# Fused attention and MLP, forward and backward in one kernel: W3 read ahead of the V prefetch, W4 in a V buffer, half of dW4 later

## The chip, the cores and the metric

One core of one Trainium2 chip. Its engines run their own instruction streams in order and meet through semaphores: PE (TensorE, matrix products into the accumulator memory PSUM; the load of its weights is shown as PEld), DVE (VectorE), ACT (ScalarE), POOL (GpSimd) and SP (SyncE). SP and POOL do almost no arithmetic here: SP issues the reads from memory into the on-chip memory, POOL issues the writes back. All transfers run on the same 16 DMA engines. The metric is device time in microseconds.

## The reference

A block for one token (D = 640) is run forward and then differentiated. Attention has 32 heads, a cache of 8192 keys and values for each and 192 numbers per key; the MLP has 1536 hidden units.

```python
def _A_ref(x, k_cache, v_cache, wq, wo):
    q = (x @ wq).reshape(B, Sq, Hq, Dh).transpose(0, 2, 1, 3)
    scores = jnp.einsum('bhqd,bhkd->bhqk', q, k) * Dh ** (-0.5)
    o = jnp.einsum('bhqk,bhkd->bhqd', _softmax(scores), v)
    return o.transpose(0, 2, 1, 3).reshape(B, Sq, Hq * Dh) @ wo
...
mod = (_silu(c) @ w_mod).reshape(c.shape[0], 6, 1, -1)
sa, ca, ga, sb, cb, gb = ...
h = _layernorm(x) * (1 + ca) + sa
x = x + ga * _A_ref(h, A_k_cache, A_v_cache, A_wq, A_wo)
h = _layernorm(x) * (1 + cb) + sb
x = x + gb * _B_ref(h, B_w1, B_w2, B_w3, B_w4)
...
_out, _vjp = jax.vjp(_f, A_x, A_k_cache, A_v_cache, A_wq, A_wo, B_w3, B_w4, c, w_mod)
return (_out, *_vjp(grad_out))
```

With one token the shifted branch inside `_B_ref` is zero, so the MLP part is `x1 + gelu(layernorm(x1) @ w3) @ w4`. Ten results are written: the block's output and the gradients of x, the K cache, the V cache, wq, wo, W3, W4, c and w_mod. The gradients of the two caches are as large as the caches (out_2 and out_3, 100 MB each), so most of the bytes are K and V in, V in once more, dK and dV out.

## The kernel before

A head's K or V is read as two tiles of 128 partitions x 32 keys x 192 numbers (1536 KB each), called (head, half). Three parts follow one another.

**Forward, heads 0 to 31** (the loop at L582, one step works on three heads at once). K is multiplied by q (`fwd_mult`), summed over the 192 numbers by PE (`fwd_ssum`), the softmax weights E are made (`fwd_exp`), K is scaled by E on ACT and DVE (`fwd_scale`, L394 and L402), and PE multiplies V with the scaled K, with a last column for E itself (`fwd_kvA`, `fwd_kvB`, L419 and L427). This gives the output of the head and a matrix that later yields the gradient of q without a further read of K. `fwd_keep` and `fwd_keepB` copy that matrix from PSUM into `MA` and `MB`; `fwd_kvK` (L435) adds the scaled K into one accumulator, kb_ps.

**The turn** (L662 to about L955). The last head's output goes through wo, the layer norm, W3, the gelu and W4, and back again to `dao_bf` (L924), the gradient of the attention's output. Only then can any gradient of a cache be made. The backward step through W3 needs W3 transposed, which PE does in 60 blocks (`w3T_some`, L678, copied from PSUM by ACT or DVE into w_t3 and w_t2); `u_mm` (L742) is the forward product with W3. `dg_some` (L143 in the trace) makes the row sums of W4 times the incoming gradient, twelve `dot`s on DVE. `dw4_some` (L816) makes the twelve blocks of W4's gradient on DVE. `woT_some` transposes the last rows of wo; `do_half` turns dao_bf into `do_pb`, the gradient of the last pair of heads' outputs.

**Backward, heads 31 to 0** (the loop at L1263; `HS` is the list of heads in that order). For each head V is multiplied by do_pb (`bwd_mult`, L131), summed by PE (L1056), dK is made by DVE (`bwd_dk`) and dV by ACT and DVE (`bwd_dv`); PF and P2h are the softmax weights, made by `bwd_pf_act` on ACT and `bwd_pf_dve` on DVE. Beside each head run jobs: `J1` holds a list per step (dwo, dW3, later wq and w_mod). `ring_load` issues the V reads as their buffers come free: a read waits for the last use of what was in the buffer. `bwd_ttr` (L985) multiplies wo's rows with dao, for the heads to come.

Buffers: `big` has five tiles, shared by K, part of the weights, and the outputs dK and dV; `fv` has three for V; `fpr` two, for the products of K and then for V; `bso` two for small outputs. A tile is reused when its last reader, a transfer too, is done.

W4 and W3 lie in three tiles, w_t0 (nine of W4's twelve blocks), w_t1 (three of W4's blocks and two of W3's five) and w_t2 (three of W3's five blocks); w_t3 takes transposed blocks. Before, all four are `big` tiles. The order of PE, DVE and ACT is pinned to the order of the program text; SP and POOL follow their program order as well. At the end of the forward loop the reads on SP stand in this order: V(30,0), V(30,1), V(31,0), W4 (nine blocks), V(31,1), wo, V(29,0), V(29,1), W4 (three blocks), W3 (two blocks), V(30,0) again, W3 (three blocks), V(30,1) again; then wo rows for the backward heads and the ring of V reads. V(31,0) and V(31,1) stay in their tiles from forward to backward.

On POOL, the writes start with the first six blocks of dW4, the two parts of dV(31,0), two writes of three dW4 blocks each, dV(31,1), dV(30,0), dV(30,1), dK(31,0), dK(31,1).

The lines on which the steps depend:

```python
        if i == HQ:
            V_b[HQ - 3] = [load_v(fpr, HQ - 3, t) for t in range(2)]
            alloc_wt(1)
            load_wt(1)
            V_b[HQ - 2] = [load_v(fv, HQ - 2, 0)]
            alloc_wt(2)
            load_wt(2)
            V_b[HQ - 2].append(load_v(big, HQ - 2, 1))
            dg_some(0, 7)
```

## Time and profile before

| | |
|---|---|
| median of 3 runs | 1402.19 us (1401.65 to 1403.26) |
| profiled execution | 1402.17 us, span 1400.4 us |
| busy share of the span | PE 61%, PEld 48%, DVE 77%, ACT 68%, POOL 8% |
| moved | 570.81 MB, 408 GB/s over the span |
| read, written | 343.08 MB, 225.91 MB |

Times in the profile are microseconds from the start of the span. A row of a timeline gives the start, the length, the engine, the line of the program, the operation, the tiles it writes and reads with their shapes, how many instructions are merged in the row, and in brackets how long the engine stood idle before it and what ended that wait. SPq rows are the issue of a transfer, not the transfer; a long one was held by its queue. A row of stretches gives, for each engine, the busy time and the number of instructions, then the granted TensorE clock (1.00 is full speed), the mean busy share of the 16 DMA engines and the rate in GB/s. A share can come out slightly over 1.

### The profile page before, as it was taken

The numbers are of one execution on the slowest core, as the hardware profiler recorded it, in microseconds if no ns is written. First come the engines' busy times: TensorE is split into PE (matmuls) and PEld (weight loads), VectorE is DVE, ScalarE is ACT, GpSimd is POOL, SyncE is SP. The second block draws the span as 40 slices with busy tenths as digits, with TensorE's granted clock in tenths as the row PEclk, the third lists the DMA queues.
The fourth block names the chain that finished last, engine by engine and source line by source line (L and its number), as shares of the span: only waits on it lengthen the run. The fifth ranks groups of instructions, "written<-read, shape, count | busy, mean of one in ns | idle before, by whom it ended". The sixth has DMA issues, their size and how long they took to land. (4 is left out here: it accounts for less than half of the span.)

```text
span 1400.4 us, 28087 instructions
## 1 busy us (share of the span) xinstructions
PE 851.4 (61%) x11512; PEld 670.5 (48%) x11512; DVE 1084.7 (77%) x1328; ACT 952.1 (68%) x2603; POOL 111.3 (8%) x202
## 2 busy tenths in 40 slices
PE   3799999999999997554657454332343443534240
PEld 3577777777777776443546343222232232323230
DVE  3678888887878886599988986777577678779794
ACT  1578887787877775575875786565666558559680
POOL 0000000000000000101110101111111111111011
PEclk9799999999999999666666657665667666666575
DMA  9999999999999999588999999999999999999997
GB/s 393 418 420 418 418 420 419 420 420 420 419 408 420 411 417 381 193 340 337 425 427 424 428 426 428 427 428 427 426 427 425 425 425 418 426 418 423 429 429 303
DMA packets 73168, 570.81 MB, mean 408 GB/s; under 512 B 6863, under 2 KB 19919, under 8 KB 32591
## 3 DMA queue, kind: packets, MB, share of 16 engines
q1 hardware_dynamic: 48736, 343.10, 59.5%
q0 software_dynamic: 24272, 225.92, 38.3%
q8 instruction: 90, 1.47, 0.4%
q14 instruction: 40, 0.32, 0.1%
q10 hardware_dynamic: 30, 0.00, 0.0%
HBM read 343.08 MB, written 225.91 MB: 406 GB/s over the span
## 5 line engine op out<-in xcount | busy, mean ns | idle before, releaser
L1074 ACT ACTIVATE dV<-do_pb,PF 128x192 bf16<-128x192 bf16 x1248 | 435.1, 440 | 80.3 <-DMA out_dram<-dK 64.9
L1056 PE MATMUL dP_ps<-V_sb,ident_bf 128*128 128x256 bf16 x1536 | 228.2, 323 | 239.9 <-DVE V_sb L131 239.9
L394 ACT ACTIVATE EK<-K_sb,E_f 128x192 bf16<-128x192 bf16 x1024 | 363.5, 442 | 8.8 <-PE kb_ps L435 3.1
L1056 PEld LDWEIGHTS <-ident_bf 128*128 128x128 bf16 x1536 | 177.4, 116 | 290.3 <-issue 171.9
L1041 DVE TENSOR_TENSOR dK<-dS,q_pb 128x6144 bf16<-128x6144 bf16 (+1 forms) x67 | 213.0, 3211 | 37.9 <-DMA out_dram<-dK 34.1
L131 DVE TENSOR_TENSOR prod<-K_sb,q_pb 128x6144 bf16<-128x6144 bf16 x64 | 214.6, 3354 | 35.4 <-DMA K_sb<-in_A_k_cache_dram 35.0
L131 DVE TENSOR_TENSOR V_sb<-V_sb,do_pb 128x6144 bf16<-128x6144 bf16 x64 | 211.9, 3350 | 6.0 <-DMA V_sb<-in_A_v_cache_dram 6.0
L419 PE MATMUL ps_a<-EK,V_sb 128*128 128x193 bf16 x2048 | 199.2, 250 | 23.1 <-DMA V_sb<-in_A_v_cache_dram 22.2
L419 PEld LDWEIGHTS <-V_sb 128*128 128x128 bf16 x2048 | 173.1, 99 | 43.0 <-DMA V_sb<-in_A_v_cache_dram 35.0
L402 DVE TENSOR_TENSOR EK<-K_sb,P2h 128x1536 bf16<-128x1536 bf16 x128 | 121.6, 951 | 0.0
L1041 DVE TENSOR_TENSOR dV<-P2h,do_pb 128x2304 bf16<-128x2304 bf16 (+1 forms) x63 | 85.0, 1375 | 45.2 <-DMA out_dram<-dV 40.0
L427 PE MATMUL ps_b<-EK,V_sb 128*64 128x193 bf16 x2048 | 111.3, 251 | 0.0
L361 PE MATMUL S_ps<-prod,ident_bf 64*64 64x256 bf16 x3072 | 100.7, 279 | 9.5 <-DVE prod L131 9.1
L361 PEld LDWEIGHTS <-ident_bf 64*64 64x64 bf16 x3072 | 84.2, 110 | 24.7 <-issue 24.1
L427 PEld LDWEIGHTS <-V_sb 128*64 128x64 bf16 x2048 | 83.6, 110 | 21.0 <-issue 21.0
L382 ACT ACTIVATE E_f<-sm_ps,negm 128x64 f32<-128x64 f32 x32 | 10.0, 314 | 83.1 <-DVE negm L380 83.1
L435 PE MATMUL kb_ps<-EK,hot_bf 128*32 128x384 bf16 x1024 | 66.0, 335 | 0.0
L1080 POOL DMA_DIRECT2D out_dram<-dV x63 | 33.7, 535 | 392.4 <-ACT dV L1074 255.5
L194 ACT CAST do_pb<-bc_ps 128x384 bf16<-128x384 f32 x15 | 7.1, 470 | 78.2 <-PE bc_ps L190 78.2
L1161 PEld LDWEIGHTS <-ident_bf 128*128 128x128 bf16 x112 | 15.2, 136 | 93.3 <-issue 91.8
L1095 POOL DMA_DIRECT2D out_dram<-dK x67 | 37.0, 553 | 192.0 <-DVE dK L1041 153.8
L1125 ACT ACTIVATE wq_o<-wq_bc,ha_f 128x1536 bf16<-128x1536 bf16 x12 | 18.5, 1566 | 49.4 <-DMA out_dram<-wq_o 49.4
(317 smaller groups left out, 828.9 us busy)
## 6 DMA issues: line engine op xcount, KB each, us to landing
V_sb<-in_A_v_cache_dram SPq DMA_DIRECT2D x126, 1536.0 KB, 16.8
K_sb<-in_A_k_cache_dram SPq DMA_DIRECT2D x64, 1536.0 KB, 19.0
out_dram<-dV POOLq DMA_DIRECT2D x63, 1536.0 KB, 21.9
out_dram<-dK POOLq DMA_DIRECT2D x63, 1536.0 KB, 22.3
wq<-in_A_wq_dram SPq DMA_DIRECT2D x3, 2560.0 KB, 34.1
wo_t<-in_A_wo_dram SPq DMA_DIRECT2D x16, 480.0 KB, 18.3
out_dram<-dwo POOLq DMA_DIRECT2D x16, 480.0 KB, 19.9
wq<-in_A_wq_dram SPq DMA_DIRECT2D x4, 1920.0 KB, 36.0
```

The lines of the kernel that those rows point to most:

```text
L131: nc.vector.tensor_tensor(out=out, in0=a, in1=b, op=ALU.mult)
L361: nc.tensor.matmul(st["S_ps"][c0 : c0 + 64, r, t * JH : (t + 1) * JH, :], lhsT=ident_bf[64 * r : 64 * r + 64, 64 * r : 64 * r + 64], rhs=p ...
L394: nc.scalar.activation(out=EK[:, jj, 0:DH], in_=K_st[h, t][:, r * JQ + jj, :], func=ACT.Copy, scale=st["E_f"][:, j : j + 1])
L402: nc.vector.tensor_tensor(out=EK[:, NA:JQ, 0:DH].rearrange("p j (d r) -> p j d r", r=2), in0=K_st[h, t][:, r * JQ + NA : (r + 1) * JQ, :]. ...
L419: nc.tensor.matmul(st["A_ps"][:, 0 : DH + 1], lhsT=V_sb[:, r * JQ + jj, a0:a1], rhs=EK[:, jj, 0 : DH + 1], start=(q == 0 and jj == 0), sto ...
L427: nc.tensor.matmul(st["B_ps"][g : g + 64, 0 : DH + 1], lhsT=V_sb[:, r * JQ + jj, b0:b1], rhs=EK[:, jj, 0 : DH + 1], start=(q == 0 and jj < ...
L435: nc.tensor.matmul(kb_ps[g : g + 32, 0 : 2 * DH], lhsT=hot_bf[:, HQ - 1 - h : 2 * HQ - 1 - h], rhs=EK[:, jj : jj + 2, 0:DH], start=(h == 0 ...
L1041: nc.vector.tensor_tensor(out=o.rearrange("p j (d r) -> p j d r", r=2), in0=pairs[:, :, None, :].to_broadcast([P, n, NP2, 2]), in1=vec.rea ...
L1056: nc.tensor.matmul(bst[h]["dP_ps"][:, t * JH : (t + 1) * JH, :], lhsT=ident_bf, rhs=V_sb[:, :, k * DS : (k + 1) * DS], start=(k == 0), sto ...
L1074: nc.scalar.activation(out=o[:, jj, :], in_=doh, func=ACT.Copy, scale=bst[h]["PF"][:, j0 + jj : j0 + jj + 1])
L1080: st2.dma_start(out=dV_hd[h][:, j0 + r0 : j0 + r1, :], in_=o[:, r0:r1, :])
L1095: st2.dma_start(out=dK_hd[h][:, j0 : j0 + n, :], in_=o[:, r0 : r0 + n, :])
```

## The change

- **Reads.** W4's nine blocks go into the `fv` buffer that V(31,0) had, and are read ahead of V(31,0), which goes into `big`. In the last forward step the rest of W4 and all of W3 are read first, and the four V tiles for the backward part after them. The order on SP becomes V(30,0), V(30,1), W4 (nine), V(31,0), V(31,1), wo, W4 (three), W3 (two), W3 (three), V(29,0), V(29,1), V(30,0), V(30,1).
- **Row sums of W4.** `dg_some` makes four at the first place and eight at the second, instead of seven and five.
- **Kept matrices.** `fwd_keep` is split. For the last head the copies into MA, Bt and MB stand later, beside the products with W3. The last head's four `fwd_kvK` groups, which stood together between the transposes, are spread: one ahead of `u_mm`, three in the tail. Two groups of eight transposes are copied by DVE instead of one, and the first of them comes as soon as du_bf is made.
- **dW4.** Six of the twelve blocks stay in the turn, with one write. The other six become two jobs, `job_dw4`, of backward steps 22 and 23, on ACT, each with a write of three blocks.
- **PF of the second head** is made on ACT together with the first one's, before `woT_some`, instead of after `bcast_dao`.
- **x's gradient columns.** `job_mid`, with the block's output, goes from step 1 to step 11; `mid_cols` from step 1 to step 2; the result of W4's product is copied from PSUM (h2_c) at step 0.

```diff
@@ -332,7 +332,7 @@
 
     def fwd_load(h, t):
         if 0 <= h < HQ and len(st[h]["V"]) == t:
-            st[h]["V"].append(load_v(big if (h, t) == (HQ - 2, 1) else fv, h, t))
+            st[h]["V"].append(load_v(big if (h, t) in ((HQ - 2, 1), (HQ - 1, 0)) else fv, h, t))
         if h + 2 < HQ and (h + 2, t) not in K_st:
             K_st[h + 2, t] = load_k(h + 2, t)
 
@@ -453,16 +453,21 @@
         k = int(2 * hp >= H_LO)
         return mm_parts[k][2][:, hp - k * H_LO // 2, :]
 
+    def fwd_keepA(h, st):
+        nc.scalar.copy(out=MA(h), in_=st["A_ps"][:, 0 : DH + 1])
+
+    def fwd_keepBt(h, st):
+        _, _, bp, _, _ = head_split(h)
+        Bt = fsm.tile([P, DH + 1], FP32, name="Bt")
+        nc.scalar.copy(out=Bt[bp : bp + 64, :], in_=st["B_ps"][64 - bp : 128 - bp, 0 : DH + 1])
+        st["Bt"] = Bt
+
     def fwd_keep(h, st):
         if h == H_LO:
             kx_cm.__exit__(None, None, None)
             mm_open("mm_hi", HQ - H_LO)
-        (a0, a1), (b0, b1), bp, ca_, cb_ = head_split(h)
-        op = 64 - bp
-        nc.scalar.copy(out=MA(h), in_=st["A_ps"][:, 0 : DH + 1])
-        Bt = fsm.tile([P, DH + 1], FP32, name="Bt")
-        nc.scalar.copy(out=Bt[bp : bp + 64, :], in_=st["B_ps"][op : op + 64, 0 : DH + 1])
-        st["Bt"] = Bt
+        fwd_keepA(h, st)
+        fwd_keepBt(h, st)
 
     def fwd_keepB(h, st):
         (a0, a1), (b0, b1), bp, ca_, cb_ = head_split(h)
@@ -528,7 +533,7 @@
         return w_t[f // W4_N][:, c0 + lo : c0 + hi]
 
     def alloc_wt(k):
-        w_t.append(flat(big_tile(f"w_t{k}")))
+        w_t.append(flat(ring_tile(fv) if k == 0 else big_tile(f"w_t{k}")))
 
     def load_wt(k):
         if k < 2:
@@ -590,18 +595,16 @@
         if p:
             fwd_wo(i - 1, st[i - 1])
         if i == HQ - 1:
-            fwd_load(HQ - 1, 0)
             alloc_wt(0)
             load_wt(0)
+            fwd_load(HQ - 1, 0)
         if i == HQ:
+            for k in (1, 2):
+                alloc_wt(k)
+                load_wt(k)
             V_b[HQ - 3] = [load_v(fpr, HQ - 3, t) for t in range(2)]
-            alloc_wt(1)
-            load_wt(1)
-            V_b[HQ - 2] = [load_v(fv, HQ - 2, 0)]
-            alloc_wt(2)
-            load_wt(2)
-            V_b[HQ - 2].append(load_v(big, HQ - 2, 1))
-            dg_some(0, 7)
+            V_b[HQ - 2] = [load_v((fv, big)[t], HQ - 2, t) for t in range(2)]
+            dg_some(0, 4)
         if pp:
             fwd_kv(i - 2, 2, st[i - 2])
         if c:
@@ -658,7 +661,7 @@
             fwd_o_head(HQ - 2)
             dve_copy(o_col_bf[:, NQC - 3 : NQC - 2], o_col_f[:, NQC - 3 : NQC - 2])
             dve_copy(o_col_bf[0:64, NQC - 2 : NQC - 1], o_col_f[0:64, NQC - 2 : NQC - 1])
-            dg_some(7, NFC)
+            dg_some(4, NFC)
     w_t.append(flat(big_tile("w_t3")))
     NB3 = JH * DH // P
 
@@ -712,10 +715,8 @@
     dot(jk, xs, xs, s3[:, 1:2])
     dot(jk, xs, cb1, s3[:, 2:3])
     w3T_some(8)
-    fwd_keep(LH, sl)
     m3 = tn[:, 0:3]
     nc.tensor.matmul(m3, lhsT=negd_mat, rhs=s3, start=True, stop=True)
-    fwd_keepB(LH, sl)
     nv = ccol(1, "nv")
     nc.vector.tensor_scalar(out=nv, in0=m3[:, 0:1], scalar1=m3[:, 0:1], scalar2=m3[:, 1:2], op0=ALU.mult, op1=ALU.add)
     std1 = ccol(1, "std1")
@@ -725,7 +726,9 @@
     v1 = ccol(1, "v1")
     nc.vector.tensor_scalar(out=v1, in0=m3[:, 0:1], scalar1=cm[:, 0:1], scalar2=m3[:, 2:3], op0=ALU.mult, op1=ALU.add)
     nc.vector.tensor_scalar(out=t1, in0=t1, scalar1=v1[:, 0:1], scalar2=None, op0=ALU.add)
+    fwd_keepA(LH, sl)
     w3T_some(8)
+    fwd_kvK(LH, 0, sl, True)
     hb_bf = ccol(NDC, "hb_bf", BF16)
     hbm = ccol(NDC, "hbm")
     r1 = ccol(1, "r1")
@@ -744,9 +747,11 @@
     u_mm(0, 4)
     nc.tensor.matmul(tn[:, 8:9], lhsT=negd_mat, rhs=s1, start=True, stop=True)
     u_mm(4, NFC)
+    fwd_keepBt(LH, sl)
     std2 = ccol(1, "std2")
     nc.scalar.activation(out=std2, in_=tn[:, 8:9], func=ACT.Sqrt, bias=eps_c[:, 0:1], scale=-1.0)
     nc.scalar.activation(out=warm, in_=eps_c, func=ACT.Exp)
+    fwd_keepB(LH, sl)
     n1_c = ccol(NDC, "n1_c")
     nc.vector.tensor_scalar(out=n1_c, in0=xs, scalar1=m3[:, 0:1], scalar2=r1[:, 0:1], op0=ALU.add, op1=ALU.mult)
     add(ao_c, ao_c, ao_ps)
@@ -777,6 +782,9 @@
     stt(deriv, deriv, 1.0, sg, ALU.subtract, ALU.mult)
     du_bf = ccol(NFC, "du_bf", BF16)
     stt(du_bf, deriv, -1.0, d_g, ALU.mult, ALU.mult)
+    w3T_some(8)
+    w3T_some(8, dve_copy)
+    fwd_kvK(LH, 1, sl, True)
     hcb = ccol(NDC, "hcb")
     mul(hcb, h1, cb1)
     g1 = ccol(NDC, "g1")
@@ -797,27 +805,24 @@
     mul(g_f, u, sg)
     g_bf = ccol(NFC, "g_bf", BF16)
     dve_copy(g_bf, g_f)
-    w3T_some(8)
+    for q, n, f in ((2, 8, act_copy), (3, 4, act_copy)):
+        w3T_some(n, f)
+        fwd_kvK(LH, q, sl, True)
     w3T_some(8, dve_copy)
-    for q, n in enumerate((8, 4, 8, 4)):
-        fwd_kvK(LH, q, sl, True)
-        w3T_some(n)
+    w3T_some(4)
     dn2_ps = bank("b", name="dn2_ps")
     for f in range(NFC):
         for i in range(NDC):
             nc.tensor.matmul(dn2_ps[:, i : i + 1], lhsT=w3T(f * NDC + i), rhs=du_bf[:, f : f + 1], start=(f == 0 and i == 0), stop=(f == NFC - 1), skip_group_check=True)
     nc.tensor.matmul(tn[:, 16:22], lhsT=negd_mat, rhs=cs, start=True, stop=True)
     dw4_n = [0]
-    W4_O = (6, 3, 3)
 
     def dw4_some(n):
         for f in range(dw4_n[0], dw4_n[0] + n):
-            tl, c0 = (w_t[2], f * D) if f < W4_O[0] else (w_t[1], W4_R * D + (f - W4_O[0]) * D)
-            nc.vector.tensor_scalar(out=tl[:, c0 : c0 + D], in0=dbo_bc, scalar1=g_f[:, f : f + 1], scalar2=None, op0=ALU.mult)
-            if f + 1 in (W4_O[0], W4_O[0] + W4_O[1], NFC):
-                m = W4_O[0] if f < W4_O[0] else W4_O[1]
-                nc.gpsimd.dma_start(out=out_7[(f + 1 - m) * P : (f + 1) * P, :].rearrange("(c p) r -> p c r", p=P), in_=tl[:, c0 - (m - 1) * D : c0 + D].rearrange("p (c r) -> p c r", r=D))
+            nc.vector.tensor_scalar(out=w_t[2][:, f * D : (f + 1) * D], in0=dbo_bc, scalar1=g_f[:, f : f + 1], scalar2=None, op0=ALU.mult)
         dw4_n[0] += n
+        if dw4_n[0] == 6:
+            nc.gpsimd.dma_start(out=out_7[0 : 6 * P, :].rearrange("(c p) r -> p c r", p=P), in_=w_t[2][:, 0 : 6 * D].rearrange("p (c r) -> p c r", r=D))
 
     kb_sb = const.tile([P, 2 * DH], FP32, name="kb_sb")
     fek_cm.__exit__(None, None, None)
@@ -895,6 +900,7 @@
         woT_next[0] += n
 
     bwd_pf_act(HS[0])
+    bwd_pf_act(HS[1])
     woT_some(2)
     dw4_some(2)
     s4 = ccol(4, "s4")
@@ -925,7 +931,7 @@
     m0d = ccol(1, "m0d")
     dve_copy(m0d, m4[:, 0:1])
     bwd_pf_dve(HS[0])
-    dw4_some(4)
+    dw4_some(3)
     psum_cm.__exit__(None, None, None)
     psum[0] = ctx.enter_context(tc.tile_pool(name="psum_b", bufs=1, space=bass.MemoryType.PSUM, reuse_waits="tile"))
     CB[0] = 2
@@ -1095,6 +1101,7 @@
             st2.dma_start(out=dK_hd[h][:, j0 : j0 + n, :], in_=o[:, r0 : r0 + n, :])
 
     dx1 = ccol(NDC, "dx1")
+    h2_c = ccol(NDC, "h2_c")
 
     def job_mid():
         x1_c = ccol(NDC, "x1_c")
@@ -1111,7 +1118,7 @@
         nc.vector.tensor_scalar(out=dx1, in0=dx1, scalar1=md[:, 0:1], scalar2=r1[:, 0:1], op0=ALU.add, op1=ALU.mult)
         add(dx1, dx1, dy_c)
         h2 = ccol(NDC, "h2")
-        add(h2, hb_c, h2_ps[:, 0:NDC])
+        add(h2, hb_c, h2_c)
         mul(dmod_c[:, 5 * NDC : 6 * NDC], dy_c, h2)
         mul(h2, h2, gb)
         add(h2, h2, x1_c)
@@ -1125,6 +1132,12 @@
             nc.scalar.activation(out=out, in_=in_, func=ACT.Copy, scale=col)
         else:
             nc.vector.tensor_scalar(out=out, in0=in_, scalar1=col, scalar2=None, op0=ALU.mult)
+
+    def job_dw4(k):
+        o = bso.tile([P, 3, D], BF16, name="dw4", tag="so")
+        for cc in range(3):
+            tsc(o[:, cc, :], dbo_bc, g_f[:, 3 * k + cc : 3 * k + cc + 1], 0)
+        st2.dma_start(out=out_7[3 * k * P : 3 * (k + 1) * P, :].rearrange("(c p) r -> p c r", p=P), in_=o)
 
     def job_dw3(i):
         o = bso.tile([P, F], BF16, name="dw3", tag="so")
@@ -1201,6 +1214,8 @@
         J1[1 + k].append(lambda hp=PS[k]: job_dwo(hp))
     for k in range(NDC):
         J1[1 + HH + k].append(lambda i=k: job_dw3(i))
+    for k in range(2):
+        J1[1 + HH + NDC + k].append(lambda k=k: job_dw4(2 + k))
 
     def add_outer(at, name, view, lo, n, col_bf, rows_f, dram, acc, first):
         J2[at].append(lambda: job_outer_load(name, view, lo, n))
@@ -1246,11 +1261,10 @@
             dq[i] = (PS[1], 2, fin_dq_mm(PS[1], 2))
 
     bwd_dv(HS[0], 0, 0, 2, w_t[3].rearrange("p (j d) -> p j d", d=DH))
-    dw4_some(5)
     bwd_dv(HS[0], 1)
+    bwd_pf_dve(HS[1])
     bcast_dao()
     q_pb[PS[0]] = pair_bc(bsm, q_bf, PS[0], "q_pb")
-    bwd_pf(HS[1])
     bwd_mult(HS[0], 0)
     ring_load()
     bwd_dv(HS[1], 0, 8)
@@ -1294,8 +1308,11 @@
             fin_c_copy(*cps.pop(i))
         if i == 0:
             mid_mm()
-        if i == 1:
+        if i == 0:
+            dve_copy(h2_c, h2_ps[:, 0:NDC])
+        if i == 2:
             mid_cols()
+        if i == NPH + 1:
             job_mid()
             dve_copy(dmod_bf[:, 2 * NDC : 6 * NDC], dmod_c[:, 2 * NDC : 6 * NDC])
         if i == NPH - 1:
```

## The prediction

> **What bounds the kernel now.** I read the page's line of transfer rates in 40 slices first, then busy time by stretches, then the timelines of the stretch that fell out.
>
> ```profile
> GB/s 393 418 420 418 418 420 419 420 420 420 419 408 420 411 417 381 193 340 337 425 427 424 428 426 428 427 428 427 426 427 425 425 425 418 426 418 423 429 429 303
> ```
> ```profile
> 560.00:580.00 20.00, 13.56 (x226) 10.44 (x227) 8.88 (x59) 9.53 (x16) 0.00 (x0) 0.66 0.26 95
> 580.00:600.00 20.00, 7.39 (x106) 5.67 (x104) 14.77 (x31) 16.16 (x45) 4.65 (x6) 0.58 0.85 322
> 600.00:620.00 20.00, 10.25 (x67) 8.21 (x66) 18.66 (x26) 10.36 (x31) 2.14 (x4) 0.67 0.89 338
> 620.00:640.00 20.00, 6.67 (x48) 5.26 (x47) 19.82 (x30) 19.97 (x55) 2.94 (x5) 0.67 0.98 384
> 640.00:660.00 20.00, 10.61 (x66) 8.30 (x66) 18.63 (x39) 8.13 (x21) 2.35 (x4) 0.67 0.73 270
> 700.00:800.00 100.00, 52.04 (x313) 44.36 (x314) 88.42 (x112) 71.17 (x188) 13.04 (x22) 0.65 1.01 426
> ```
> The last columns are the granted TensorE clock, the DMA share and GB/s. The transfers set the time: they run at about 420 GB/s in the first slices and at 418 to 429 in those from 665 us to the last but one, a share of 1.01 in the row quoted. Bytes do not change, so only the hole between counts. Against 426 GB/s a 20 us row loses 20 x (1 - rate/426): 15.5, 4.9, 4.1, 2.0 and 7.3, together **33.8 us**. An edit is worth what it fills of that.
>
> Why the hole is there:
>
> ```profile
> 541.53 0.82 DVE L143 CUSTOM_DVE_ANT_0 w_t<-w_t,dbo_bc 128x640 bf16<-128x640 bf16 x1 [4.71 <-DMA w_t<-in_B_w_dram]
> 547.70 0.59 PE L473 MATMUL sm_ps<-rowsum,ones_mat_f 128*128 128x2 f32 x2 [6.19 <-DVE ao_c L134]
> 557.48 1.54 PE L419 MATMUL ps_a<-EK,V_sb 128*128 128x193 bf16 x16
> 563.99 0.40 PE L678 MATMUL t_ps<-ident_bf,w_t 128*128 128x128 bf16 x2 [4.61 <-DMA w_t<-in_B_w_dram]
> 582.37 0.23 DVE L140 SCALAR_TENSOR_TENSOR dao_bf<-h,md,zd 128x5 bf16<-128x5 f32 x1
> 545.42 5.73 SPq L330 DMA_DIRECT2D V_sb<-in_A_v_cache_dram  x1
> 577.89 0.37 SPq L856 DMA_DIRECT2D V_sb<-in_A_wo_dram  x1
> ```
> The last forward read is issued at 545.42 and no read follows until 577.89. Output can start only behind dao_bf (582.37). That chain starts at 563.99, when the transposes get the last part of W3, which stands in SP's queue behind V(29,0), V(29,1) and V(30,0). Ahead of it, DVE waits 4.71 us for W4, and PE 6.19 us for the row sums behind it (seven dots before ao_c).
>
> **Part by part.**
>
> *W3 ahead of V.* W3's last part now follows wo, W4's rest and W3's first part, and three V tiles of 1.573 MB come behind it. At 418 GB/s each takes 3.76 us: 11.3 us, so it lands at 563.9 - 11.3 = 552.6. Bounds: 0 gained, if the queue clogs, and 12, where the work ahead becomes the wait. That work: W4 swaps places with V(31,0), one tile earlier, so DVE's 4.71 shrink to about 1 (537.7); four dots (0.82 us and a read of the sum, 0.87 in steps) end at 541.2, PE's 6.19 us vanish, and the row-sum total and the last head's matmuls behind it start at about 541.7. They need V(31,0), now where W4 was (landed 541.5), and V(31,1), unmoved; in as long as before (547.7 to 559.0, slowed at first) they end at 553, and faster warm. The eight later dots end at 551.5. All three meet near **552.6**: 11.3 us earlier.
>
> ```profile
> 537.23 5.07 SPq L539 DMA_DIRECT2D w_t<-in_B_w_dram  x1
> 543.14 0.38 SPq L539 DMA_DIRECT2D w_t<-in_B_w_dram  x1
> 533.94 8.40 ACT L394 ACTIVATE EK<-K_sb,E_f 128x192 bf16<-128x192 bf16 x24
> 532.00:536.00 4.00, 4.00 (x63) 2.98 (x59) 2.33 (x9) 2.46 (x8) 0.00 (x0) 1.00 0.70 259
> ```
> Its tile takes over K(31,0), read until 16 of the 24 ACT scalings are done (539.5), so it can go out about 3.5 us before its old 543.14 unless the queue, which held W3's first part for 5.07 us, holds longer now. What that costs: behind W4's rows of 1280 bytes the rate fell to 259 GB/s. The 480 + 480 + 768 + 1152 KB (2.95 MB) of wo, W4 and W3 now stand together; at 259 instead of 418 they take 4.3 us more, and W3 lands at 556.9 (a rival below). The V tiles that step back land by the old 567; DVE's first use of one comes at 598 by the steps below, 31 us of cover. [...]
>
> *Kept matrices later.*
>
> ```profile
> 565.37 0.59 PE L717 MATMUL turn_ps<-s,negd_mat 128*128 128x3 f32 x2
> 567.01 0.36 DVE L134 TENSOR_TENSOR MB_all<-ps_b,Bt 64x193 f32<-64x193 f32 x1 [1.69 <-ACT Bt L464]
> 567.40 0.29 DVE L720 TENSOR_SCALAR nv<-turn_ps 128x1 f32<-128x1 f32 x1
> 568.80 0.69 PE L742 MATMUL ps_a<-hb_bf,w_t 128*128 128x1 bf16 x20 [1.97 <-DVE hb_bf L140]
> 572.64 0.83 PE L435 MATMUL kb_ps<-EK,hot_bf 128*32 128x384 bf16 x8
> ```
> nv waited for the B half (to 567.37); its own matmul L717 ends at 565.96. So nv moves up 1.4 us, and L742 1.1, since one kb group (0.83 us, in the 1.97 us PE idled) now stands before it. The moved copies lie beside L742. The tail has one kb group less and a second transpose copy on DVE; of the 0.83 us I take 0.6, since the copies behind PE still pace part of it. Together 1.7 (0 to 3): the chain is **13.0 us** earlier, dao_bf at 569.4.
>
> *dW4 and PF.*
>
> ```profile
> 587.24 1.57 DVE L816 TENSOR_SCALAR w_t<-dbo_bc,g_f 128x640 bf16<-128x640 bf16 x5
> 594.72 0.23 DVE L879 CAST P2h<-PF 128x128 bf16<-128x128 f32 x1 [4.65 <-ACT PF L875]
> 593.23 0.55 POOL L1080 DMA_DIRECT2D out_dram<-dV  x1 [2.78 <-ACT dV L1074]
> 594.72 9.78 ACT L1074 ACTIVATE dV<-do_pb,PF 128x192 bf16<-128x192 bf16 x28
> 603.57 3.65 SPq L330 DMA_DIRECT2D V_sb<-in_A_v_cache_dram  x2
> 583.08 1.76 PE L944 MATMUL h_ps<-g_bf,w_t 128*128 128x1 bf16 x60
> 629.53 2.25 ACT L1125 ACTIVATE dwo<-dao_bc,o_col_f 128x640 bf16<-128x640 bf16 x3
> ```
> DVE sheds five dW4 rows (1.57 us), one more ahead of dV (0.3), and the 4.65 us wait for the second head's PF, now made early on ACT. DVE is **6.5 us** further forward, 19.5 in all; ACT's dV keeps only the 13.0. The read at 603.57 goes into the buffer that now holds W4, so it waits for L944 (end 584.84) and not for V(31,0): 571.8. The two dW4 writes of 480 KB leave POOL's queue ahead of dV(31,1) and come back at heads 22 and 23 behind those heads' dV. Their 0.98 MB still move, so they add no time to the sum; ACT pays twice 2.25 us for them (three rows of 640, as in the dwo row), hidden while the transfers are behind; uncovered, 4.5 us.
>
> *x's columns later.*
>
> ```profile
> 639.69 0.17 DVE L131 TENSOR_TENSOR x_c<-ao_c,mod_c 128x5 f32<-128x5 f32 x1
> 643.89 3.35 DVE L131 TENSOR_TENSOR V_sb<-V_sb,do_pb 128x6144 bf16<-128x6144 bf16 x1
> 652.08 21.11 SPq L330 DMA_DIRECT2D V_sb<-in_A_v_cache_dram  x4
> ```
> The work from 639.69 to 643.89 (4.2 us) delays the products that free the V buffers, and with them the read at 652.08. It goes to head 11, where DVE waits on transfers anyway; without that cover it costs 4.2 there. The added h2_c copy is one 0.15 us row. DVE is 23.7 us ahead from head 2.
>
> *Sum.*
>
> ```profile
> V_sb<-in_A_v_cache_dram SPq DMA_DIRECT2D x126, 1536.0 KB, 16.8
> ```
> I lay the bytes end to end at 426 GB/s from 567, each 2 us behind its issue. By then the forward reads drain in both kernels: the last is issued by 551.15 and a V read lands 16.8 us later in the median. With the old issue times this leaves 30.1 us empty; the rows say 33.8, so rate dips add 3.7. With the new times (Wo's read 564.9; V 571.8; the dW4 and first dV writes 13.3 earlier; dV(31,1) 580.2; dV(30,0) 584.5, when ACT has 8 of the 28, and dV(30,1) 591.5 with all; the rest 19.5 and then 23.7 earlier) four gaps stay: 2.2 before dW4, 0.9 before dV(30,0), 2.5 before the next Wo read, 3.0 before head 2's V reads: 8.7, with dips 12.4. Gain 33.8 - 12.4 = 21.4. The profiled execution took 1402.17 us (span 1400.4), as good as the median of 1402.19, so **1381 us**.
>
> **The rivals.**
>
> *PE stays warm.*
>
> ```profile
> 572.00:576.00 4.00, 3.66 (x35) 1.91 (x33) 3.65 (x26) 2.12 (x3) 0.00 (x0) 0.50 0.00 0
> 573.41 1.03 PE L678 MATMUL t_ps<-ident_bf,w_t 128*128 128x128 bf16 x8
> 576.80 0.61 PE L678 MATMUL t_ps<-ident_bf,w_t 128*128 128x128 bf16 x8 [0.15 <-ACT w_t L194]
> ```
> The clock is still 0.50 at 576, 12 us after the 4.61 us wait. Eight transposes take 1.03 us then, 0.61 at 576.8. With the chain's 56 transposes as seven such pieces, 0.42 us each makes up to 3 us where ACT's copies don't hold them: 16 us in all, gaps 5.7, time **1378**. [...]
>
> *The queue clogs.* W3 at 556.9: the chain 8.7 us earlier, gaps 13, time **1385**.
>
> *W3 isn't earlier at all* (its issue, or V(31,0) behind W4, comes late): only the 1.7 us and DVE's gains remain; laid out again, the gaps are 20.0 and the time **1392**. Against it: the built order has W3 in front, and its tile is free at 539.5.
>
> *The end isn't the transfers' alone.* If a late stretch is set by ACT or DVE, the lead is used up there and the time stays near **1402**. Against it: the share of 1.01 and the even late slices quoted first.
>
> *Slower: the new dW4 jobs stall ACT.*
>
> ```profile
> 1137.70 0.55 POOL L1132 DMA_DIRECT2D out_dram<-dw  x1
> 1170.49 0.55 POOL L1132 DMA_DIRECT2D out_dram<-dw  x1
> DMA to landing us min/median/max: 16.2/23.3/29.6
> ```
> Each job needs one of two tiles, last written to memory two jobs earlier. Behind it on ACT stands the next head's dV, and POOL's queue waits for that. If neither tile is free, each job costs up to 29.6 + 2.25 us, two 63.7, the time 1381 + 64 = **1445**. It decides once a job comes sooner than 29.6 us after the write two jobs back; the writes two heads apart lie some 60 us apart (33 from one to the next here), so 30 us of cover.
>
> **How the numbers follow.** My forecast has 0.45 (its own range 1377 to 1385); PE warm 0.17, clogged queue 0.16, W3 not earlier 0.12, no gain 0.05, slower 0.05. The range 1375 to 1392 takes in the first four and leaves out no gain, slower and about a fifth of the case at its upper end. Faster by over 0.2% (2.8 us, what a measurement can tell): 0.45 + 0.17 + 0.16 + 0.12 = 0.90; within 0.05; slower 0.05.
>
> **What would show it.** W3's wait at L678 near 552.6, no long PE idle before it; dao_bf near 569.4; the 560:580 row well over 250 GB/s, the 640:660 row over 400; DVE without the 4.65 us wait; the same rates after 660, all shifted by about 21 us. I am wrong if W3 lands after 557, if a write waits for a buffer between 580 and 640, or if ACT waits at the new jobs.

## The result, and the profile after

The changed kernel takes 1381.68 us (median of 4 runs, 1379.52 to 1384.65) against 1401.92 us before in the same session: a ratio of 0.9855, 95% interval 0.9835 to 0.9876. Five more runs of it, beside new runs of the kernel before, gave 1380.73 us and 0.9847 (0.9833 to 0.9861). The prediction was 1381 us. The profiled execution took 1382.4 us (span 1380.5).

The stretch that fell out, by windows (us of the window, busy time of PE, PEld, DVE, ACT and POOL, granted TensorE clock, DMA share, GB/s), of the kernel after:

```profile
560.00:580.00 20.00, 11.66 (x209) 9.26 (x206) 16.38 (x51) 13.53 (x35) 2.61 (x4) 0.67 0.92 331
580.00:600.00 20.00, 11.32 (x71) 8.91 (x69) 17.14 (x24) 12.47 (x36) 1.60 (x3) 0.67 0.94 364
600.00:620.00 20.00, 7.60 (x48) 5.73 (x48) 19.90 (x22) 19.97 (x56) 2.94 (x5) 0.67 0.83 316
620.00:640.00 20.00, 11.97 (x74) 9.93 (x73) 19.76 (x23) 11.23 (x30) 2.35 (x4) 0.67 0.99 397
640.00:660.00 20.00, 18.20 (x120) 16.09 (x120) 19.66 (x37) 13.84 (x40) 1.65 (x3) 0.67 1.01 427
700.00:800.00 100.00, 51.59 (x304) 42.66 (x303) 83.98 (x100) 71.22 (x193) 12.28 (x21) 0.64 1.01 426
```

By the prediction's own measure, 20 x (1 - rate/426), the five rows lose 4.5, 2.9, 5.2, 1.4 and 0 us: 13.9 where 33.8 were lost before. Behind 660 the rate is what it was. So 19.9 us of the hole are filled, and the two profiled executions differ by 1402.17 - 1382.4 = 19.8 us. That they agree within 0.1 us is partly luck: worked out in the same way, the profiled executions of the other runs below are up to 3.4 us (i1) longer than their rates say. One row of 100 us says the same in one number, and the experiments below are compared by it. First the kernel before, then the kernel after:

```profile
560.00:660.00 100.00, 48.46 (x507) 37.89 (x507) 80.76 (x180) 64.14 (x164) 12.08 (x19) 0.65 0.74 282
```
```profile
560.00:660.00 100.00, 60.75 (x518) 49.92 (x515) 92.83 (x153) 71.03 (x193) 11.15 (x19) 0.67 0.94 367
```

100 x (1 - 282/426) = 33.8 us lost, and 100 x (1 - 367/426) = 13.8.

The chain that opens the output, in the timeline of the kernel after (start, duration, engine, line; in brackets the idle time before and what ended it):

```profile
538.04 0.83 DVE L143 CUSTOM_DVE_ANT_0 w_t<-V_sb,dbo_bc 128x640 bf16<-128x640 bf16 x1 [0.75 <-DMA V_sb<-in_B_w_dram]
541.90 0.38 PE L478 MATMUL sm_ps<-rowsum,ones_mat_f 128*128 128x2 f32 x2
553.02 0.29 PE L681 MATMUL t_ps<-ident_bf,w_t 128*128 128x128 bf16 x2 [0.36 <-DMA w_t<-in_B_w_dram]
554.71 0.29 DVE L721 TENSOR_SCALAR nv<-turn_ps 128x1 f32<-128x1 f32 x1 [0.48 <-PE turn_ps L719]
555.97 0.65 PE L745 MATMUL ps_a<-hb_bf,w_t 128*128 128x1 bf16 x20 [0.40 <-DVE hb_bf L140]
567.55 0.23 DVE L140 SCALAR_TENSOR_TENSOR dao_bf<-h,md,zd 128x5 bf16<-128x5 f32 x1
570.01 0.33 SPq L330 DMA_DIRECT2D V_sb<-in_A_v_cache_dram  x1
```

DVE's wait for W4 is 0.75 us (it was 4.71), PE no longer waits for the row sums (6.19), and the wait for the last part of W3 ends at 553.0 instead of 564.0. dao_bf comes 14.8 us earlier, where the prediction had 13.0. The V read that went out at 603.57 goes out at 570.01.

Not all of it stayed. Further on, the same timeline has two waits that the kernel before did not have there, and a third that was 1.06 us there:

```profile
579.76 2.56 DVE L1047 TENSOR_TENSOR dV<-P2h,do_pb 128x4608 bf16<-128x4608 bf16 x1 [2.79 <-ACT q_pb L194]
583.95 7.02 ACT L1080 ACTIVATE dV<-do_pb,PF 128x192 bf16<-128x192 bf16 x20 [1.28 <-DMA out_dram<-w_t]
590.10 0.16 DVE L197 COPY c_bc<-c_ps 128x2 f32<-128x2 f32 x1 [2.51 <-PE c_ps L147]
```

The first names ACT's copy of q_pb, which dV does not read. The trace has another event at the right time: the dW4 write was issued at 569.18 and took 10.5 us to land, so it landed at 579.7. In e3 and e4 below the same instruction waits 2.07 and 1.11 us, and there the profile names the landing of a write from w_t. In a second profile of the same kernel (e8) this write, issued at 570.08, landed after 6.2 us, and dV(30,0) starts at 578.12 without a wait. The second wait, on ACT, is for the second part of dV(31,0), issued at 572.86 and landed 11.0 us later. The third is for a small sum that stands behind dP's matmuls in PE's order.

### The profile page after: what moved, and what is told of

The parts are those of the page before. It is cut to its first block, busy times and chain, and to the rows that moved or that the text cites. A ratio compares the mean times of both kernels' runs of the same rounds, so it can differ in the third digit from the quotient of the medians.

```text
span 1380.5 us, 28092 instructions
## 1 busy us (share of the span) xinstructions
PE 848.3 (61%) x11512; PEld 666.4 (48%) x11512; DVE 1084.2 (79%) x1324; ACT 955.7 (69%) x2608; POOL 110.8 (8%) x202
## 5 line engine op out<-in xcount | busy, mean ns | idle before, releaser
L1062 PE MATMUL dP_ps<-V_sb,ident_bf 128*128 128x256 bf16 x1536 | 233.1, 327 | 253.4 <-DVE V_sb L131 253.4
## 6 DMA issues: line engine op xcount, KB each, us to landing
K_sb<-in_A_k_cache_dram SPq DMA_DIRECT2D x64, 1536.0 KB, 19.8
```

The costliest lines, as they stand in the source:

```text
L1062: nc.tensor.matmul(bst[h]["dP_ps"][:, t * JH : (t + 1) * JH, :], lhsT=ident_bf, rhs=V_sb[:, :, k * DS : (k + 1) * DS], start=(k == 0), sto ...
```

## The experiments

For each run, the time is the median, and "lost" is worked out from its row of 560 to 660 us as above. The kernel after has 13.8 us lost in one profile and 11.0 in the other (e8 below), so differences in lost time under some 3 us are not told apart by one profile. The runs come from four sessions, in which the kernel before had medians of 1401.9 us (after), 1402.2 (e1 to e4), 1402.8 (e5 to e7, i1) and 1401.8 (e8, i2), so times of different sessions compare to about 1 us.

| run | time, us | ratio to before (95%) | lost, us |
|---|---|---|---|
| before | 1402.2 | 1 | 33.8 |
| after | 1381.7 | 0.9855 (0.9835 to 0.9876) | 13.8 |
| e1: old order of reads | 1392.4 | 0.9929 (0.9916 to 0.9941) | 24.2 |
| e2: new order of reads alone | 1394.4 | 0.9951 (0.9937 to 0.9964) | 24.4 |
| e3: kept matrices as before | 1382.1 | 0.9862 (0.9849 to 0.9875) | 14.1 |
| e4: x's columns as before | 1385.5 | 0.9882 (0.9870 to 0.9895) | 16.0 |
| e5: second PF late | 1386.6 | 0.9882 (0.9859 to 0.9904) | 17.8 |
| e6: all of dW4 early | 1386.4 | 0.9881 (0.9855 to 0.9908) | 15.3 |
| e7: W4 behind V(31,0) | 1384.7 | 0.9867 (0.9844 to 0.9891) | 16.2 |
| e8: after again | 1380.7 | 0.9847 (0.9833 to 0.9861) | 11.0 |
| i1: both products first | 1382.2 | 0.9847 (0.9821 to 0.9873) | 11.7 |
| i2: and the sums for c first | 1378.9 | 0.9837 (0.9823 to 0.9850) | 7.5 |

**e1, the reads in their old order.**

```diff
         if i == HQ - 1:
+            fwd_load(HQ - 1, 0)
             alloc_wt(0)
             load_wt(0)
-            fwd_load(HQ - 1, 0)
         if i == HQ:
-            for k in (1, 2):
-                alloc_wt(k)
-                load_wt(k)
             V_b[HQ - 3] = [load_v(fpr, HQ - 3, t) for t in range(2)]
-            V_b[HQ - 2] = [load_v((fv, big)[t], HQ - 2, t) for t in range(2)]
-            dg_some(0, 4)
+            alloc_wt(1)
+            load_wt(1)
+            V_b[HQ - 2] = [load_v(fv, HQ - 2, 0)]
+            alloc_wt(2)
+            load_wt(2)
+            V_b[HQ - 2].append(load_v(big, HQ - 2, 1))
+            dg_some(0, 7)
```

> The changed kernel with the reads in their old order (V(31,0) ahead of W4, V(29) and V(30,0) ahead of W3, W4 back in its own tile, seven dots ahead); the late copies, the later columns, PF and the dW4 jobs stay. My theory: the transfers set the end, and W3 read ahead is worth the 11.0 us by which it landed earlier. Then W3's wait at L678 ends again near 564, dao_bf is written near 578.5, and the layout of the transfers with the changed kernel's own issue times moved by 11.0 us has 21.6 us empty instead of 10.6: 1382 + 11 = 1393 us. Rival 1, the reads are the whole of the gain and the other edits are worth nothing: 1402 us. Rival 2, the transfers can catch up a late chain, because the other edits keep them busy: 1386 us or less.

Measured: 1392.43 us. Rows of its windows and its timeline:

```profile
560.00:660.00 100.00, 59.71 (x557) 47.46 (x558) 87.92 (x161) 67.49 (x176) 10.61 (x18) 0.63 0.83 323
```
```profile
564.54 0.39 PE L683 MATMUL t_ps<-ident_bf,w_t 128*128 128x128 bf16 x2 [4.87 <-DMA w_t<-in_B_w_dram]
581.04 0.23 DVE L140 SCALAR_TENSOR_TENSOR dao_bf<-h,md,zd 128x5 bf16<-128x5 f32 x1
```

The wait for W3 is back with its 4.87 us, and 100 x (1 - 323/426) = 24.2 us are lost instead of 13.8. The order of the reads is worth 10.7 us of time in this kernel, about what W3 gained in landing against the kernel before (11.0 us; 11.5 against e1). dao_bf, at 581.04, is 1.3 us ahead of the kernel before (582.37) although W3's wait ends 0.6 us later (564.54 against 563.99): the other edits give the chain 1.9 us, with the clock at 0.50 from 564 to 572 in both.

**e2, the new order of reads alone, in the kernel before.** The diff is e1's the other way round, on the kernel before.

> The kernel before with the new order of reads alone (and W4 in the V buffer, four dots ahead). My theory: W3 lands near 553, the chain is 11 us earlier and nothing else; the layout goes from 30.1 us empty to 18.9, so 1402 - 11 = 1391 us; DVE's 4.65 us wait for PF is there again, and the stretch before x's columns still has a gap of several us. Rival 1 (the reads are all of it): 1382 us. Rival 2 (what is won at the start is lost again at the old waits behind it, PF and x's columns): over 1396 us.

Measured: 1394.4 us (1392.65 to 1400.21), between my theory and the second rival. Its row of 560 to 660 us has 322 GB/s. Timeline:

```profile
570.26 0.23 DVE L140 SCALAR_TENSOR_TENSOR dao_bf<-h,md,zd 128x5 bf16<-128x5 f32 x1
577.69 7.01 ACT L1072 ACTIVATE dV<-do_pb,PF 128x192 bf16<-128x192 bf16 x20 [3.41 <-DMA out_dram<-w_t]
586.49 0.23 DVE L877 CAST P2h<-PF 128x128 bf16<-128x128 f32 x1 [7.51 <-ACT PF L873]
```

The chain is 12.1 us earlier, and part of that lead goes with the next waits: ACT waits 3.41 us until a write from w_t has landed, and DVE's old wait for PF grows from 4.65 to 7.51 us, since PF stands behind those dV on ACT. So the parts are not additive: the reads alone gain 7.8 us (1402.2 - 1394.4), everything else alone 9.8 (e1), and both together 20.5.

**e3, the kept matrices as before.** The copies and the kb groups go back to their old places.

```diff
+    fwd_keep(LH, sl)
     m3 = tn[:, 0:3]
     nc.tensor.matmul(m3, lhsT=negd_mat, rhs=s3, start=True, stop=True)
+    fwd_keepB(LH, sl)
     nv = ccol(1, "nv")
...
-    fwd_keepA(LH, sl)
     w3T_some(8)
-    fwd_kvK(LH, 0, sl, True)
```

> The changed kernel with the copies of the last head's kept matrices and the kb groups in their old places. As predicted, they are worth 1.7 us of the chain: dao_bf near 569.3 and 1383.5 us. Rival, read from the changed kernel, whose chain from W3's landing to dao_bf is 3.8 us shorter than before (14.5 against 18.4): dao_bf near 571.4, and by the layout 14.4 us empty for 10.6, 1386 us. Second rival: most of these 3.8 us come from TensorE's clock, which stays up because it no longer waits, and not from the copies: dao_bf under 568.5 and 1382 us.

Measured: 1382.14 us. Timeline of e3, to be read against nv and L745 of the kernel after:

```profile
553.19 0.28 PE L681 MATMUL t_ps<-ident_bf,w_t 128*128 128x128 bf16 x2 [0.28 <-DMA w_t<-in_B_w_dram]
556.09 0.29 DVE L723 TENSOR_SCALAR nv<-turn_ps 128x1 f32<-128x1 f32 x1
557.47 0.65 PE L745 MATMUL ps_a<-hb_bf,w_t 128*128 128x1 bf16 x20 [2.17 <-DVE hb_bf L140]
```

The copies do about what the prediction said they do on the chain: nv is 1.4 us later with the copies in their old places, L745 1.5, of which 0.2 are a later end of W3's wait. dao_bf is written at 570.9, between the first two expectations, while the time is that of the second rival. Of its 3.3 us against 567.55 a part goes with the clock: 0.50 at 560 to 564 in e3, 0.82 in the kernel after. Against e5, which has the new order of the copies and, like e3, a clock of 0.50 from 560 on (there still at 568 to 572, in e3 up to 564), dao_bf is 1.4 us later (570.86 against 569.42); the prediction had 1.7. And the 3.3 us become 1.1 us at the first dK write (599.31 against 598.22) and 0.5 us of time: the later waits named above differ too, of which DVE's is 2.07 us in e3 and 2.79 after, and c's 1.06 and 2.51. The part is worth little here, and how little can't be told from the noise.

**e4, x's gradient columns at the second step again.**

```diff
-        if i == 0:
-            dve_copy(h2_c, h2_ps[:, 0:NDC])
-        if i == 2:
+        if i == 1:
             mid_cols()
-        if i == NPH + 1:
             job_mid()
```

> The changed kernel with x's gradient columns back at the second step. My theory: the 4.2 us of DVE's work delay the products that free the V buffers, as before: issues behind 615 come 4.2 us later, the layout has 14.8 us empty for 10.6, 1386 us. Rival: by the second step the transfers are already behind the engines, so that the work is hidden there too: 1382 us.

Measured: 1385.54 us, as expected. DVE's products of heads 1 and 2, in the timeline of the kernel after and then of e4:

```profile
601.25 6.62 DVE L131 TENSOR_TENSOR V_sb<-V_sb,do_pb 128x6144 bf16<-128x6144 bf16 x2
621.96 6.62 DVE L131 TENSOR_TENSOR V_sb<-V_sb,do_pb 128x6144 bf16<-128x6144 bf16 x2
```
```profile
598.62 6.62 DVE L131 TENSOR_TENSOR V_sb<-V_sb,do_pb 128x6144 bf16<-128x6144 bf16 x2
620.29 0.17 DVE L131 TENSOR_TENSOR x_c<-ao_c,mod_c 128x5 f32<-128x5 f32 x1
624.48 6.62 DVE L131 TENSOR_TENSOR V_sb<-V_sb,do_pb 128x6144 bf16<-128x6144 bf16 x2
```

From one head to the next it takes 20.7 us without the columns and 25.9 with them: 5.2 us. Of these, 4.2 us lie from 620.29 to 624.48, the work that the prediction counted; the 1.0 us ahead of it is `mid_cols`, which the edit also brings back by one step. Together they cost 3.9 us of time (1385.54 against 1381.68).

**e5, the second head's PF late again.**

```diff
-    bwd_pf_act(HS[1])
     woT_some(2)
...
     bwd_dv(HS[0], 1)
-    bwd_pf_dve(HS[1])
     bcast_dao()
     q_pb[PS[0]] = pair_bc(bsm, q_bf, PS[0], "q_pb")
+    bwd_pf(HS[1])
     bwd_mult(HS[0], 0)
```

> The changed kernel with the second head's PF made late again (behind the broadcasts on ACT, its copy on DVE behind them). In the changed kernel DVE reaches dV(30,0) early and waits there 2.79 us for a write to land (start 579.76). My theory: ACT makes PF near 580, the product on V(31,0), which starts at 573.62, waits for it, and dV(30,0) starts 3.8 us later (583.6); by the layout about 1385.5 us. As predicted (4.65 us all kept): 1386.5 us. Rival: the wait for the landing hides it and the time is that of the changed kernel, 1382 us.

Measured: 1386.59 us. In its timeline:

```profile
569.42 0.23 DVE L140 SCALAR_TENSOR_TENSOR dao_bf<-h,md,zd 128x5 bf16<-128x5 f32 x1
582.14 0.23 DVE L884 CAST P2h<-PF 128x128 bf16<-128x128 f32 x1 [6.37 <-ACT PF L880]
```

DVE waits 6.37 us for PF, and its 2.79 us in front of dV(30,0) are gone in return. The rival, that this hides it, falls: the time is 4.9 us longer than after, near the 4.65 us that the prediction gave this edit.

**e6, all of dW4 early.** Seven rows ahead of the first dV and five behind its first half, written in three pieces, no dW4 jobs later.

```diff
-    dw4_some(3)
+    dw4_some(4)
     psum_cm.__exit__(None, None, None)
...
     bwd_dv(HS[0], 0, 0, 2, w_t[3].rearrange("p (j d) -> p j d", d=DH))
+    dw4_some(5)
     bwd_dv(HS[0], 1)
...
-    for k in range(2):
-        J1[1 + HH + NDC + k].append(lambda k=k: job_dw4(2 + k))
```

> The changed kernel with all of dW4 made on DVE before the first dV's second half and written at once, as before (no dW4 jobs at later heads). As predicted, DVE is 1.9 us later (five rows 1.57, one more row 0.3), the 0.98 MB moved early fill what they delay, and the time is that of the changed kernel within 2 us: 1382 to 1383.6 us. Rival 1: the two writes stand ahead in the queue and make the later tiles wait, over 1385 us. Rival 2, the jobs at the later heads cost ACT time (4.5 us uncovered): without them the kernel is faster, 1378 us.

Measured: 1386.44 us: the first rival. Timeline of e6:

```profile
576.90 7.01 ACT L1083 ACTIVATE dV<-do_pb,PF 128x192 bf16<-128x192 bf16 x20 [3.43 <-DMA out_dram<-w_t]
585.33 2.56 DVE L1050 TENSOR_TENSOR dV<-P2h,do_pb 128x4608 bf16<-128x4608 bf16 x1 [3.74 <-DMA out_dram<-w_t]
```

DVE's rows cost what the prediction gave them (five in 1.60 us, one more in 0.30). The rest goes with waits. The dV tiles reuse the buffers of w_t, and ACT (3.43 us) and DVE (3.74) wait until writes out of w_t have landed. By their issue and landing times these are not the two new writes: the first dW4 write, issued at 571.07, took 5.7 us (ACT's wait ends at 576.90), and the second part of dV(31,0), issued at 575.09, took 10.1 (DVE's ends at 585.33). The six blocks that stay early lie in w_t1; my reading is that this keeps w_t1 taken, so that each dV gets a tile that comes free later. No run tests that apart. At the other end of the edit, the timeline of the kernel after shows the two jobs, each of three rows on ACT, with no idle time in front of them:

```profile
1167.87 2.25 ACT L1132 ACTIVATE dw<-dbo_bc,g_f 128x640 bf16<-128x640 bf16 x3
1197.22 2.25 ACT L1132 ACTIVATE dw<-dbo_bc,g_f 128x640 bf16<-128x640 bf16 x3
```

**e7, W4 behind V(31,0) again**, in its own tile, W3 still ahead of the prefetch.

```diff
         if i == HQ - 1:
+            fwd_load(HQ - 1, 0)
             alloc_wt(0)
             load_wt(0)
-            fwd_load(HQ - 1, 0)
```

> The changed kernel with W4 behind V(31,0) again and in its own tile; W3 stays ahead of the V prefetch. My theory: DVE's dots and with them the row sums and the last head's matmuls end one tile (3.5 us) later, near 556, so that W3, landed near 553, no longer sets the chain; the V read that goes into W4's buffer goes out near 588 instead of 570. By the layout 14.0 us empty for 10.6: 1385 us, and DVE has its wait of over 4 us for W4 back. Rival 1: the delay is taken up by the waits for landings behind it, as most of the 3.3 us of the kept copies were: 1382 us. Rival 2: the read that goes out late costs its whole 3.7 us on top: 1389 us.

Measured: 1384.68 us, near the 1385 of my theory. Timeline of e7:

```profile
542.01 0.82 DVE L143 CUSTOM_DVE_ANT_0 w_t<-w_t,dbo_bc 128x640 bf16<-128x640 bf16 x1 [4.55 <-DMA w_t<-in_B_w_dram]
555.88 1.53 PE L419 MATMUL ps_a<-EK,V_sb 128*128 128x193 bf16 x16
557.50 0.38 PE L681 MATMUL t_ps<-ident_bf,w_t 128*128 128x128 bf16 x4
573.27 0.23 DVE L140 SCALAR_TENSOR_TENSOR dao_bf<-h,md,zd 128x5 bf16<-128x5 f32 x1
```

The last head's matmuls now end at 557.4, the transposes start behind them at 557.5 and wait for no transfer. With W4 late, W3, which landed at 553.0 in the kernel after, is early in vain for 4.5 us. "All three meet" needed the swap of W4 too. dao_bf is 5.7 us later than after, the time 3.0 us longer, though the runs of the two overlap (1383.31 to 1385.78, after up to 1384.65).

**i1, both products of the last head first.** The three later waits point to an order with less of them.

```diff
     bwd_mult(HS[0], 0)
+    bwd_mult(HS[0], 1)
     ring_load()
     bwd_dv(HS[1], 0, 8)
     dve_copy(do_bf[:, 3 * PS[0] : 3 * PS[0] + 3], do_ps[:, 400:403])
-    bwd_mult(HS[0], 1)
     c_first = fin_c(PS[0], 1)
```

> The changed kernel with both products of the last head ahead of dV(30,0), so that DVE works on V(31,1) (3.35 us) in the 2.79 us in which it waited for a write to land, and the sums for c come behind less of TensorE's work (2.51 us wait). My theory: DVE's later work, up to the first dK, comes 4 to 5 us earlier, the V read of 589.97 near 585.5, and the layout has 5.6 us empty for 10.6: 1377 us. Rival 1: only one of the two waits goes (8.1 us empty): 1379.5 us. Rival 2: ACT's dV(30,1), which waits for a landing and is written at 591.3 in any case, sets what follows: 1382 us.

Measured: 1382.21 us, no gain, where 1377 was expected. The time is rival 2's, but not its cause: ACT waits for no landing here. DVE's wait in front of dV(30,0) is gone, that for c's sums is not, as in rival 1, and in this profile dao_bf was written only at 569.39 (timeline of i1):

```profile
589.34 0.16 DVE L197 COPY c_bc<-c_ps 128x2 f32<-128x2 f32 x1 [2.33 <-PE c_ps L147]
592.64 0.68 DVE L1090 TENSOR_REDUCE dP<-dP_ps 128x64 f32<-128x512 f32 x1
```

**i2, the sums for c ahead of the second product.**

```diff
     bwd_mult(HS[0], 0)
-    ring_load()
-    bwd_dv(HS[1], 0, 8)
     dve_copy(do_bf[:, 3 * PS[0] : 3 * PS[0] + 3], do_ps[:, 400:403])
-    bwd_mult(HS[0], 1)
     c_first = fin_c(PS[0], 1)
+    bwd_mult(HS[0], 1)
+    ring_load()
+    bwd_dv(HS[1], 0, 8)
```

> As in i1, and the sums for c ahead of the product on V(31,1), so that their matmul stands ahead of the second half of dP's on TensorE. In i1 DVE waited 2.33 us at c's copy for it (589.34). My theory: the wait goes, dP's reduction comes about 2 us earlier than in i1 (590.6) and with it the first dK, the product on V(30,0) and the read of Wo; the loss of the 600 to 620 row falls from 4.2 to 2.2 us, and the time is 1379.5 us. Rival: dP itself, not the sums, is what DVE waits for next, or ACT's copy of kb's sums holds the broadcasts: 1382 us.

Measured: 1378.89 us (1377.16 to 1379.39), beside 1380.73 (1379.03 to 1381.85) of the kernel after in the same session. Timeline and windows of i2:

```profile
584.82 0.16 DVE L197 COPY c_bc<-c_ps 128x2 f32<-128x2 f32 x1
588.11 0.69 DVE L1090 TENSOR_REDUCE dP<-dP_ps 128x64 f32<-128x512 f32 x1
```
```profile
560.00:660.00 100.00, 59.44 (x520) 49.40 (x519) 98.05 (x154) 75.50 (x202) 11.69 (x20) 0.67 0.99 394
```

The wait is gone, as expected. dP's reduction comes 4.5 us earlier than in i1 (1.7 of them because dao_bf was written at 567.7 and not at 569.4), and 7.5 us are lost for 11.0 to 13.8; the row of 600 to 620 us, at 387 GB/s, loses 1.8, where 2.2 were expected. i2 is the fastest of all these kernels, by 1.8 us over the changed one; the intervals of the two ratios still overlap, so the gain is not certain.

**e8, the changed kernel once more.**

> The changed kernel once more. In its first profile TensorE's granted clock was 1.00 at 564 to 568 and dao_bf was written at 567.55; the two runs e5 and i1, whose program is the same up to there, had 0.50 from 560 on and 569.4. If the clock falls in this stage in some executions and not in others, this profile shows one of the two: dao_bf at 567.5 or at 569.4, and the time stays within 2 us of 1381.7 in either case, since the 3.3 us of the kept copies came to nothing too. Rival: the change had a good execution, and cold it takes 1384 us or more.

Measured: 1380.73 us, within the 2 us. Its profile shows neither of the two times but one between (timeline of e8):

```profile
568.46 0.23 DVE L140 SCALAR_TENSOR_TENSOR dao_bf<-h,md,zd 128x5 bf16<-128x5 f32 x1
590.84 0.69 DVE L1090 TENSOR_REDUCE dP<-dP_ps 128x64 f32<-128x512 f32 x1
```

dao_bf is 0.9 us later than in the first profile, and yet less time is lost (11.0 us for 13.8), since DVE's 2.79 us wait is not there (the write landed earlier) and that for c's sums is 1.38 us. Here a microsecond in the chain was worth no more than the waits behind it allowed.

## Why the prediction was right

- *The measure.* The transfers set the end, and the filled hole was the gain: 19.9 us filled by the rows, 19.8 us between the profiled executions. The residue of 12.4 us (8.7 of gaps and 3.7 of dips) was measured as 13.8 and 11.0. The sum came out closer than its parts. Windows of the kernel after:

```profile
589.00:592.00 3.00, 1.06 (x11) 0.89 (x9) 1.90 (x6) 2.33 (x7) 0.53 (x1) 1.00 0.57 145
605.00:613.00 8.00, 7.25 (x48) 5.48 (x46) 7.97 (x11) 8.00 (x24) 0.53 (x1) 0.74 0.56 179
```

  The gap before the next Wo read (issued at 609.66) was to be 2.5 us and is 4.6 (3.9 in e8). The one before dV(30,0), 0.9 us, is not there (435 GB/s from 580 to 589); 2.0 us are lost at 589 to 592 instead, around the write of dV(30,1) (591.26), and none there in e8. Before head 2's V reads (630.26) 3.0 us were to be lost, and 1.3 are, at 632 to 636. So it is in part luck that the total fits. No run shows the 2 us that the layout put between the issue of a transfer and its bytes: in the kernel before, the Wo read issued at 577.89 is followed by 154 GB/s already at 579.0 to 579.5.
- *W3 ahead of V.* W3 was to land at 552.6 and landed at 553.0; DVE's first dot was to start at 537.7 and started at 538.0; PE's 6.19 us wait is gone. e1 gives the worth, 10.7 us, and the rival "W3 not earlier" (1392) was the right time for that kernel: 1392.4. The three paths did meet there: in the kernel after the last dot ends at 551.9, the last head's matmuls at 552.0 and W3's wait at 553.0.
- *The queue does not clog.* The rival of 1385 us falls. The dip is there, only earlier; windows of the kernel after:

```profile
528.00:532.00 4.00, 3.55 (x78) 2.87 (x72) 3.84 (x12) 3.31 (x10) 0.00 (x0) 1.00 0.69 242
532.00:536.00 4.00, 4.00 (x70) 3.11 (x64) 2.59 (x8) 2.00 (x7) 0.00 (x0) 1.00 0.96 362
```

  One row of 4 us at 242 GB/s, as one row at 259 before; wo, W4's rest and W3 right behind it ran at 362 and more. The dip came 4 us earlier, as W4's nine blocks did (issued at 520.90, before at 525.01), and what follows them did not widen it.
- *Kept matrices.* The 1.4 us at nv and 1.1 at L742 were measured as 1.4 and 1.5, the whole term of 1.7 as 1.4 at a similar clock (e3 against e5). The size was right on the chain; that the chain's microseconds are time was not: 3.3 us of dao_bf came to 0.5 (e3), which is within the noise.
- *dW4 and PF.* The 4.65 us of PF were right (e5: 4.9). The dW4 term was mis-sized: 1.9 us of DVE rows, measured 4.8 (e6), because the term had only the rows and not the waits of ACT and DVE for the tiles of w_t. Undone one at a time the two edits cost 4.9 and 4.8 us, and the prediction had 6.5 for both; together they were not undone.
- *DVE's lead.* 19.5 us were predicted. By dP's reduction it was 16.9 and 19.5 in the two profiles of the kernel after (593.39 and 590.84), with dao_bf 1.8 and 0.9 us earlier than forecast: the chain gave more, the waits behind it took it back. The reference is this row of the kernel before:

```profile
610.30 0.69 DVE L1084 TENSOR_REDUCE dP<-dP_ps 128x64 f32<-128x512 f32 x1
```

- *x's columns.* 4.2 us predicted; 4.2 of DVE's time measured (5.2 with `mid_cols`), and 3.9 of the kernel's (e4).
- *My own condition for being wrong*, a write's buffer waited for between 580 and 640, was met, in small: ACT waited 1.28 us, up to 583.95, for a tile whose write had not landed, and DVE 2.79 us, up to 579.76, just ahead of that stretch. The layout had none of these waits, but it had dao_bf 1.8 us later than this profile. The profile without DVE's wait lost 2.8 us less (13.8 against 11.0), and both lie inside the range.
- *The slower rival* (dW4 jobs that stall ACT) is excluded by the two rows at 1167.87 and 1197.22, which have no wait before them.

## What to carry to other kernels

Where transfers set the end, as here (426 GB/s in the stretch from 700 to 800 us of both kernels), cost an edit by how much of the hole in their rate it fills (19.9 us filled, 19.8 us gained), and undo each edit alone from the final kernel: the parts interlock (7.8 and 9.8 us apart, 20.5 together). An earlier chain was worth only what the waits behind it let through (12.1 us of dao_bf were 7.8 us of time in e2, 3.3 us were 0.5 in e3), so look for the writes that must land before a buffer is used again (3.43 us on ACT and 3.74 on DVE in e6), and for small sums that stand behind long matmul groups (2.51 us in the kernel after). Of the 4.8 us of e6 the instructions were 1.9; the rest went with waits for buffers.
